# Reordering the start of a fused convolution and gated-MLP kernel: where loads, casts and hand-over marks stand, and two PSUM tiles for the last set

## The chip, the cores and the metric

One NeuronCore of a Trainium2 chip. The metric is device time in microseconds (us) of one execution; runs are compared on the same chip and in the same rounds. TensorE is "PE" in the profile, VectorE "DVE", ScalarE "ACT", GpSimd "POOL", SyncE's DMA queue "SPq".

## The reference

```python
def reference(x, weight, moe_w_in, moe_w_out):     # cut to what matters
    w = softmax(weight, axis=-1)                   # 8 heads, 7 taps
    # causal 7-tap convolution of x [8, 4096, 192], one weight row per group of 24 channels
    y = conv(x, w).reshape(32768, 192)
    h = y @ moe_w_in                               # 192 -> 2048
    return (h * cos(h)) @ moe_w_out                # 2048 -> 192
```

## The kernel before

Two batches of rows are worked at once, in the upper and lower 64 rows of the array. A string tells the order of work. Each letter is one step, and the recording keeps that order on every engine.

- `U`: 6 matmuls of 64x512 give one h tile (three PSUM tiles, of two banks each). `S`: its cosine on ACT. `M`: h times cosine on DVE, which frees the h tile.
- `d`: 8 matmuls of 64x192 into the two accumulators. Sixteen `d` make a set; `x`, `y` copy its two accumulators out.
- `C`, `c`, `e`: the two halves of a convolution pair on TensorE, then its eviction by ACT and its transposes on the DMA queue.
- `p`: GpSimd casts x for a later pair, and the x for the one after it is loaded.
- `k`: the next job of a list: casts of weights, loads.

Below, "the eleventh d" is the d with index 10 of the first set, and U16 is the first U of the second token tile. It needs the transposes of the second conv pair made in the fill.

The two halves of an accumulator pair change over at fixed d. A memset on GpSimd, the "mark", stands between, so that the matmuls on one half of the array wait for those on the other:

```python
    def changeover(end):
        ins = nc.gpsimd.memset(mark, 0.0)
        order(ins, end)                            # waits for the last matmul of the old side
        return ins                                 # the next d waits for it
    # ... in down(k, j), after step j:
        if j < 15 and TURNS[(j + 1) // 2][0] != flip:
            turns[k] = changeover(end)             # after steps 3, 9 and 13
```

The mark stands in GpSimd's program order, behind whatever cast was recorded before it (in the profile before it ran at 29.43 us, behind four casts begun at 27.63). The start, the "fill", and the end before the change:

```python
    load_w2(0)
    load_w2(1)                                     # both halves of w_out, early in the queue
    # ... cut ...
    def later():                                   # the jobs of "k"
        yield from (lambda q=q: cast_w1(1, q) for q in range(NCH))
        yield cast_pair
        yield from (lambda q=q: cast_w1(2, q) for q in range(NCH))
        yield cast_pair
        yield lambda: load_ahead(2)                # x for the third tile
        yield from (lambda q=q: cast_w1(3, q) for q in range(NCH))
        yield from (lambda c=c, q=q: cast_w2(c, q) for c in range(2) for q in range(4))
    # ... cut ...
    fill("kkkUSMUSMUSMkUSMUSMkkkUSCceMUSMUSMkUSMkUSCceMUSMkkkkkkkkkkkUSMU")
    emit("dddSMdUdMpSUdSdMUdSMdUdMSCcpUedSdMCcdedMUdpSdUyxUMS")
    for k in range(1, NSETS - 2):
        emit("dddSMdUdMSUdSdMUdSMdUdMSUdSdMCcdedMUdpSdUyxUMS")
    last = h_pool.tile([128, 2, T], FP32, name="h")
    last = [last[:, k, :] for k in range(2)]
    emit("dddMSdUdMSUdSdMUdSMdMM" + "tttt" + "dddddtttttt" + "ddxytttttt" + "xy")
```

## Time and profile before

| | before |
|---|---|
| time, median of 3 runs (range) | 723.93 us (723.11 to 724.34) |
| span of the profiled run | 721.9 us |
| TensorE busy in 40 to 710 us | 100% |
| TensorE idle in 10-20, 20-30, 30-40 us | 2.6, 2.6, 2.0 us |
| a set in steady state (first d to first d) | 10.9 us |

How to read it: a kernel whose TensorE is never idle for 670 us cannot win there by moving work. Only the first 40 us and the last 11 us can give anything.

### The profile page before, as it was taken

The page shows a single profiled execution, that of the slowest core. Times are in us where ns is not written, and L with a number is a line of the kernel's source. Part 1 is how long each engine was busy: PE and PEld are TensorE (multiplying, and loading weights), DVE is VectorE, ACT ScalarE, POOL GpSimd, SP SyncE. Part 2 cuts the span into 40 slices and gives each one's busy share as a digit, 9 for nine tenths or more (in the row PEclk, how much of TensorE's full clock was granted, in tenths as well). Part 3 has the DMA queues.
Part 4 walks back from the last instruction along what each step waited for, and adds up shares of the span by engine and source line. Part 5 has one row for each costly group of instructions (what it writes and reads, how often), then busy time and mean ns, then how long its engine had stood idle before and what let it go on. Part 6 is the DMA issues. An engine that isn't in the chain of part 4 may idle for free.

```text
span 721.9 us, 27691 instructions
## 1 busy us (share of the span) xinstructions
PE 707.8 (98%) x12370; PEld 527.0 (73%) x12370; DVE 640.9 (89%) x593; ACT 589.4 (82%) x641; POOL 95.0 (13%) x344
## 2 busy tenths in 40 slices
PE   7799999999999999999999999999999999999997
PEld 5477777777777777777777777777777777777776
DVE  5779899999889989898898998998998999999994
ACT  5788888888888888888888888888888888777773
POOL 4520111110110111111101111101101100000000
PEclk9999999999999999999999999999999999999999
DMA  9976443552616236254452352526253321011102
GB/s 227 248 120 151 87 93 93 115 132 63 158 40 157 75 83 158 66 126 109 120 121 77 94 136 83 138 59 158 50 146 85 84 62 55 25 45 46 46 24 67
DMA packets 126435, 72.58 MB, mean 101 GB/s; under 512 B 52524, under 2 KB 124780, under 8 KB 126316
## 3 DMA queue, kind: packets, MB, share of 16 engines
q1 hardware_dynamic: 125482, 70.23, 40.2%
q8 instruction: 96, 1.57, 0.9%
q10 hardware_dynamic: 834, 0.59, 0.3%
q14 instruction: 23, 0.19, 0.1%
HBM read 33.48 MB, written 25.17 MB: 81 GB/s over the span
## 4 chain that ended last, share of the span: by engine, by line
PE 95%; DMA 2%; DVE 1%; ACT 1%; issue 0%; ACTq 0%; POOL 0%; POOLq 0%
PE h L287 49%; PE acc L287 46%; DVE g L397 1%; DMA cT<-ct 1%; DMA xw<-in_x_dram 1%; ACT cos L392 0%; ACT ct L345 0%; POOL xb L161 0%; ACTq L80 0%; PE acc L487 0%; DVE osb L434 0%; ACT cT L490 0%; ACT osb L434 0%; ACT cT L491 0%; ACTq L104 0%
## 5 line engine op out<-in xcount | busy, mean ns | idle before, releaser
L397 DVE TENSOR_TENSOR g<-h,cos 128x1024 bf16<-128x1024 f32 x512 | 603.9, 1220 | 29.9 <-ACT cos L392 23.2
L392 ACT ACTIVATE cos<-h 128x1024 bf16<-128x1024 f32 x512 | 511.2, 1024 | 109.5 <-PE h L287 90.8
L287 PEld LDWEIGHTS <-g 64*128 64x128 bf16 x8192 | 353.4, 94 | 103.9 <-POOL mark L297 4.0
L287 PE MATMUL acc<-w,g 64*128 64x192 bf16 x8064 | 415.8, 243 | 1.2 <-POOL mark L297 1.2
L287 PE MATMUL h<-cT,w 64*128 64x512 bf16 x3072 | 407.0, 376 | 5.7 <-DVE g L397 3.4
L287 PEld LDWEIGHTS <-w 64*128 64x128 bf16 x3072 | 147.3, 94 | 82.6 <-issue 7.5
L297 POOL MEMSET mark<- 1x1 f32 x192 | 16.9, 88 | 601.4 <-PE acc L287 592.8
L434 DVE COPY osb<-acc 128x384 f32<-128x384 f32 x63 | 35.1, 558 | 40.2 <-PE acc L287 40.2
L161 POOL CAST xb<-xw 128x512 bf16<-128x512 f32 (+1 forms) x112 | 64.7, 607 | 15.6 <-DMA xw<-in_x_dram 14.4
L345 ACT CAST ct<-h 112x1024 bf16<-112x1024 f32 (+2 forms) x54 | 53.6, 992 | 6.0 <-PE h L287 2.4
L287 PE MATMUL h<-xb,band 64*128 64x192 bf16 (+11 forms) x940 | 34.9, 212 | 0.4 <-DVE xb L161 0.3
L434 ACT COPY osb<-acc 128x384 f32<-128x384 f32 x63 | 29.8, 473 | 5.7 <-PE acc L287 5.7
L287 PEld LDWEIGHTS <-band 64*128 64x128 bf16 x1008 | 31.6, 95 | 1.4 <-issue 1.0
L235 POOL CAST w<-xw 128x512 bf16<-128x512 f32 x12 | 7.0, 614 | 2.0 <-DMA xw<-in_moe_w_in_dram 1.9
L183 PE MATMUL acc<-unit 128*112 128x112 bf16 x76 | 5.8, 256 | 1.3 <-POOL unit L166 1.3
L183 PEld LDWEIGHTS <-unit 128*112 128x112 bf16 x76 | 5.6, 170 | 1.4 <-POOL unit L166 1.3
L287 PE MATMUL h<-w,g 64*128 64x192 bf16 x128 | 5.9, 243 | 0.3 <-POOL mark L297 0.3
L245 POOL CAST w<-xw 128x384 bf16<-128x384 f32 x8 | 3.7, 507 | 1.8 <-DMA xw<-in_moe_w_out_dram 1.8
L196 ACT ACT_TABLE_LOAD x1 | 1.3, 1283 | 2.6 <-issue 2.6
L216 ACT CAST band<-acc 128x448 bf16<-128x448 f32 x1 | 0.5, 532 | 2.7 <-PE acc L215 2.7
L434 DVE COPY osb<-h 128x384 f32<-128x384 f32 x1 | 0.6, 559 | 2.4 <-ACT osb L434 2.4
L161 DVE CAST xb<-xw 128x512 bf16<-128x512 f32 (+1 forms) x2 | 0.9, 485 | 1.4 <-DMA xw<-in_x_dram 1.4
(37 smaller groups left out, 19.9 us busy)
## 6 DMA issues: line engine op xcount, KB each, us to landing
out_dram<-osb SPq DMA_DIRECT2D x63, 384.0 KB, 2.6
xw<-in_x_dram SPq DMA_DIRECT2D x62, 384.0 KB, 6.9
xw<-in_x_dram SPq DMA_DIRECT2D x7, 336.0 KB, 4.4
xw<-in_moe_w_in_dram SPq DMA_DIRECT2D x4, 512.0 KB, 7.7
xw<-in_moe_w_out_dram SPq DMA_DIRECT2D x2, 768.0 KB, 6.4
cT<-ct SPq DMA_TRANSPOSE x68, 2.7
xw<-in_moe_w_in_dram SPq DMA_DIRECT2D x8, 128.0 KB, 7.0
xw<-in_x_dram SPq DMA_DIRECT2D x6, 96.0 KB, 6.8
```

Source lines behind the costliest of these rows:

```text
L161: copies[j % len(copies)](out=xbs[p][:, s0:s1], in_=src)
L183: nc.tensor.matmul(out=acc[0][0:W, 0:W], lhsT=unit, rhs=unit, start=True, stop=True)
L196: nc.scalar.activation(out=wex, in_=wq, func=AF.Exp)
L216: nc.scalar.copy(out=band[:, :, V:W], in_=spread)
L235: copy(out=w1[:, q, c * CW:(c + 1) * CW], in_=staged[1, c][:, q, :])
L245: nc.gpsimd.tensor_copy(out=w2[:, c * n:(c + 1) * n, :][:, fs, :], in_=staged[2, c][:, fs, :])
L287: ins = nc.tensor.matmul(out=o, lhsT=w, rhs=r, start=start, stop=stop, skip_group_check=True)
L297: ins = nc.gpsimd.memset(mark, 0.0)
L345: copy(out=ct[0:W, 0:n].rearrange("p j s c -> p s j c"), in_=ps[0:W, :, 0:n * L].rearrange("p s (j c) -> p s j c", c=L))
L392: nc.scalar.activation(out=cos, in_=hs[n], func=AF.Sin, bias=math.pi / 2.0, scale=1.0)
L397: nc.vector.tensor_tensor(out=g, in0=hs.pop(n), in1=cs.pop(n), op=ALU.mult)
L434: copy(out=osbs[k][:, 2 * bank:2 * bank + 2, :].rearrange("p a d -> p (a d)"), in_=src[:, 0:2 * D])
```

## The change

Intent: take away TensorE's waits in the fill. Half of w_out is loaded behind the first pair of transposes, x for the third tile behind the second pair. The second of two additional conv pairs moves from the first set to the second. In the last set the two accumulators get an h tile each, and three `d` are moved ahead of the last `U`.

```diff
     load_w2(0)
-    load_w2(1)
@@ later()
         yield cast_pair
-        yield lambda: load_ahead(2)
+        yield lambda: load_w2(1)
         yield from (lambda q=q: cast_w1(3, q) for q in range(NCH))
-        yield from (lambda c=c, q=q: cast_w2(c, q) for c in range(2) for q in range(4))
+        yield from (lambda q=q: cast_w2(0, q) for q in range(4))
+        yield lambda: load_ahead(2)
+        yield from (lambda q=q: cast_w2(1, q) for q in range(4))
@@
-    fill("kkkUSMUSMUSMkUSMUSMkkkUSCceMUSMUSMkUSMkUSCceMUSMkkkkkkkkkkkUSMU")
-    emit("dddSMdUdMpSUdSdMUdSMdUdMSCcpUedSdMCcdedMUdpSdUyxUMS")
-    for k in range(1, NSETS - 2):
+    fill("kkkUSMUSMUSMkUSMUSMkkkUSCceMUSMkUSMkUSMkkkUSCceMUSMkkkkkUSMU")
+    fill("dddSMdkkUdMkkSUdSdMUdSMdUpdMSUdSdMCcdedMUdpSdUyxUMS")
+    emit("dddSMdUdMSUdSdMUdSMdUdMSCcpUedSdMCcdedMUdpSdUyxUMS")
+    for _ in range(NSETS - 4):
         emit("dddSMdUdMSUdSdMUdSMdUdMSUdSdMCcdedMUdpSdUyxUMS")
-    last = h_pool.tile([128, 2, T], FP32, name="h")
-    last = [last[:, k, :] for k in range(2)]
-    emit("dddMSdUdMSUdSdMUdSMdMM" + "tttt" + "dddddtttttt" + "ddxytttttt" + "xy")
+    last = [h_pool.tile([128, 2, T], FP32, name="h")[:, 0, :] for _ in range(2)]
+    emit("dddMSdUdMSUdSdMdddUdSMdMM" + "tttt" + "ddtttttt" + "ddxytttttt" + "xy")
```

## The prediction

> **What bounds the kernel now.** I read the page first, then the table of windows, then waits, chain and timeline of the first 45 us and of the end. Letters are the kernel's own: U is one "up" block (6 matmuls of 64x512 into an h tile), S its cosine on ACT, M its product on DVE, d one "down" step (8 matmuls of 64x192), C/c the two halves of a convolution pair, e its eviction and transposes, p a cast of x. A set is 16 d. Columns of the windows are busy us per engine, then granted clock, DMA share, GB/s.
>
> ```profile
> PE 707.8 (98%) x12370; PEld 527.0 (73%) x12370; DVE 640.9 (89%) x593; ACT 589.4 (82%) x641; POOL 95.0 (13%) x344
> ...
> 10.00:20.00 10.00, 7.40 (x90) 3.93 (x92) 8.33 (x9) 7.88 (x11) 5.40 (x10) 1.00 1.08 262
> 20.00:30.00 10.00, 7.36 (x122) 4.32 (x120) 9.06 (x9) 8.59 (x11) 7.18 (x16) 1.00 1.15 286
> 30.00:40.00 10.00, 7.97 (x157) 6.02 (x155) 5.21 (x5) 5.15 (x6) 2.33 (x5) 0.83 1.17 197
> ...
> 100.00:200.00 100.00, 100.00 (x1742) 76.87 (x1740) 91.13 (x84) 84.75 (x93) 12.51 (x47) 1.00 0.43 105
> ```
>
> From 40 us to 710 us TensorE is never idle: nothing in the change can win there. What is loose is the fill (2.6 us idle in each of 10-20 and 20-30, 2.0 in 30-40, plus a lowered clock) and some 11 us at the end. The waits and the timeline of the fill say where:
>
> ```profile
> PE h L287 <- DMA cT<-ct: 2.0, 1, 2.0
> ...
> 27.63 1.86 POOL L245 CAST w<-xw 128x384 bf16<-128x384 f32 x4 [0.34 <-DMA xw<-in_moe_w_out_dram]
> 28.56 2.52 SPq L372 DMA_TRANSPOSE cT<-ct  x2
> 29.43 0.09 POOL L297 MEMSET mark<- 1x1 f32 x1
> 29.57 0.50 PE L287 MATMUL acc<-w,g 64*128 64x192 bf16 x8 [0.98 <-POOL mark L297]
> 32.58 1.17 POOL L161 CAST xb<-xw 128x512 bf16<-128x512 f32 x2 [3.06 <-DMA xw<-in_x_dram]
> 34.72 0.82 PE L287 MATMUL h<-cT,w 64*128 64x512 bf16 x6 [2.02 <-DMA cT<-ct]
> 36.27 0.09 POOL L297 MEMSET mark<- 1x1 f32 x1 [2.52 <-PE acc L287]
> ```
>
> The fifth d waits 0.98 us for a mark (a memset by which GpSimd hands the accumulator's halves over), which stood behind the w_out casts. The 17th U (U16, first of the second token tile) waits 2.02 us for transposes, issued only at 28.56, because four x loads for the third tile are issued at 25.81 ahead of them. Then the clock falls:
>
> ```profile
> 35.00:36.00 1.00, 1.00 (x17) 0.77 (x15) 0.00 (x0) 0.42 (x1) 0.00 (x0) 0.73 1.13 212
> 36.00:37.00 1.00, 1.00 (x32) 0.95 (x30) 0.36 (x1) 0.60 (x1) 0.71 (x3) 0.50 1.10 220
> 37.00:38.00 1.00, 1.00 (x7) 0.38 (x4) 0.86 (x1) 0.96 (x1) 0.44 (x1) 0.50 1.14 213
> 38.00:39.00 1.00, 1.00 (x16) 0.96 (x14) 0.00 (x0) 0.73 (x2) 0.00 (x0) 0.56 1.11 223
> ...
> 717.99 0.48 ACT L434 COPY osb<-h 128x384 f32<-128x384 f32 x1 [1.92 <-PE h L287]
> 718.50 0.56 DVE L434 COPY osb<-h 128x384 f32<-128x384 f32 x1 [2.39 <-ACT osb L434]
> ```
>
> 0.73, 0.50, 0.50, 0.56 are a half clock from about 35.46 to 38.87. The last two lines are the end: DVE's last copy waits for ACT's, though it reads another bank.
>
> [...] the 3.41 us before 35.46 were not wholly idle, only 2.0 us of them (40% busy)[...]; 11.56 to 14.98 was 62% busy and kept its clock. [...] transposes issued by 31.08 land around 35 because the x loads are ahead. [...]
>
> **The change part by part.**
> 1. *w_out's second half and its four casts go later.* The mark after the fourth d now stands ahead of those casts, after the first four, which end at 27.30; the fourth d ends at 27.95, so the mark is hidden under U13 (27.77 to 28.60). Gain 0.98 us. The second half is needed only at the ninth d.
> 2. *x for the third tile goes behind the second pair of transposes.* U16's wait goes. Check of the new rate: U13 ends 28.60, U14 after one d at about 28.9, U15 30.2, U16 at 31.6 instead of 34.72. U16 needs M13, which in the trace ends at 30.9. For the queue I work from the starts of consumers: w_out's halves land at 25.4 and 27.6, the x tile at 32.5, the transposes at about 35.0. A pair of transposes takes some 2.1 us of queue (estimate: 32.5 to 35.0 less a small x load). Order after: w_out 0, transposes, w_out 1, transposes, x. Transposes land near 30.5, before 31.6. Gain 2.03 us.
> 3. *The half clock after it.* Between 35.54 and 39.92 the chain has 0.60 for a d that costs 0.33, 2.14 for a conv half and a U that cost 1.45, 1.00 for two d that cost 0.66: 1.30 us lost, to be had back if the clock stays up.
> 4. *The x tile now lands later, and a mark stands behind its casts.* GpSimd's order after is: mark, four w_out casts, two casts of this x, mark for the eleventh d. All queue work that stood before the x tile still stands there and one pair of transposes is added: 32.46 + 2.1 = 34.5 (33.7 to 34.9). Two casts 1.17, mark and semaphores 0.2: the eleventh d can start near 35.9. Without that wait it would start at 33.3 (U16 31.6, d 0.33, U17 0.65 more, with M14 done at about 32.2). So a new TensorE stall of 2.6 us (1.9 to 3.0) takes the place of the old one.
> 5. *The clock again.* If windows lie as before (32.05 to 35.46), TensorE is idle from 33.3 to 35.46, 2.16 of 3.41 us, 37% busy, a little less than what halved the clock before. I give it 0.7. Cost: 35.9 to 38.87 at half speed, 1.5 us, so 1.05 in expectation.
> 6. *Second extra conv pair one set later.* Its matmuls (0.65 us for 40) leave the first set and come back in the second; total TensorE work is the same. In the second set each wait on M has 0.2 to 0.4 us of slack in steady state, so at most 0.2 us is lost there; after a stall DVE is ahead, so I take 0.
> 7. *The last set.* Two h tiles instead of one let DVE's last copy wait for TensorE and not for ACT: 718.50 becomes 717.99, gain 0.5. Three d moved ahead of the last U hide one exposed mark (711.14 to 711.39, 0.25), but that U ends at 709.6 instead of 708.7, its S and M (1.02 and 1.22) end near 712.1, and the d that needs it would come at 711.95: 0.2 given back. Two tiles leave U only one free h tile, but the last U waits for M508, ended at 707.4, and the first final-set step for M510, ended 709.98, both in time. Net 0.5.
>
> Sum: -0.98 - 2.03 - 1.30 + 2.6 + 1.05 + 0 - 0.5 = -1.16 us. 723.93 - 1.16 = 722.8. I shade it to 722.5, because step 4 rests on a queue estimate and errors there are more often in the new order's favour (the DMA queue was nearly idle for 1 us, at 33 to 34, in the old order; a queue without that pause lands x sooner).
>
> **The rivals.**
> A. *Clean gain.* x lands early enough (by 32, or the mark is reached otherwise) and steps 4 and 5 vanish: -4.3 - 0.5 = -4.8, 719.1 us. For it: that is evidently the intent, DMA moves 286 GB/s here and the old pause may go. Against: the x loads alone run at some 215 GB/s in the 1 us windows of this queue and cannot start before the transposes are through.
> B. *Stall without clock loss.* Step 4 as worked out, but the window straddles it[...]: -4.31 + 2.6 - 0.5 = -2.2, 721.7 us. For it: 62% busy kept the clock. Against: 37% is below the 40% that lost it.
> C. *Swap for nothing.* Stall of 3.0 with the clock halved, and a stall of a few tenths in the heavier second set: -4.31 + 3.0 + 1.5 + 0.3 - 0.2 = +0.3, 724.2 us. For it: the transposes of this trace have pauses of 1 us in them. Against: the tail gain is nearly certain.
> D. *DVE as the bound in the fill*: DVE is 9.06 of 10 busy in 20-30, so TensorE freed of its waits would catch up with M. Against: U14 to U17 need M11 to M14, ended at about 28.5, 29.6, 30.9 and 32.2, each 0.3 us or more before its U.
>
> **Range and chances.** The centre is between the expected sum and B. Eight times in ten I expect 720.2 to 724.0: the low end is a stall of about 1 us and a kept clock, the high end rival C. The whole fill idle after 11.85 us is 6.5 us, under 1%, so 2% (14.5 us) either way could come only from something I have not seen: 0.01 faster, 0.98 within, 0.01 slower.
>
> **What would show it.** Step 1: the fifth d starts before 29.0 with no wait on a mark. Step 2: U16 starts at about 31.6 with no wait on transposes. Step 4: the waits name the mark before the eleventh d, 1.9 to 3.0 us, with the x cast just before it starting at 34 to 35. Step 5: the clock column is 0.5 from about 35.5 to 38.9. Step 6: TensorE 100% busy in the second set. Step 7: the last ACT and DVE copies start together, and the end follows 0.5 us sooner. Wrong would be: no stall at the eleventh d (rival A), or a half clock anywhere else in the fill, or U idle for h tiles in the last set.

The forecast's sum came to -1.16 us, 722.8, shaded to 722.5. That a stretch with little TensorE work brings a half clock, and the chance of 0.7 in step 5, were estimates from the one profile of before: about 40% busy in 32.05 to 35.46 us, ahead of the half clock, and 62% in 11.56 to 14.98, after which the clock stayed full. Step 5's "windows" are such stretches of 3.41 us.

## The result, and the profile after

The changed kernel took 722.12 us (median of 4; 721.75 to 723.30) against 724.13 us for the kernel before (4 runs), ratio 0.9975, 95% interval 0.9957 to 0.9994. A repetition of five rounds on another chip gave 723.02 against 724.38 us, ratio 0.9979 (0.9966 to 0.9991). A ratio here is the mean time of one kernel's fast runs over that of the other's of the same rounds, so it is not quite the ratio of the medians.

The windows of the changed kernel (busy us of PE, PEld, DVE, ACT, POOL; then granted clock, DMA share, GB/s), to be held against those of before:

```profile
10.00:20.00 10.00, 7.46 (x91) 3.97 (x90) 8.29 (x9) 7.83 (x11) 4.88 (x9) 1.00 1.08 259
20.00:30.00 10.00, 8.69 (x132) 4.66 (x129) 8.31 (x8) 8.42 (x11) 6.72 (x15) 1.00 1.17 255
30.00:40.00 10.00, 7.57 (x126) 5.51 (x123) 5.87 (x5) 5.09 (x6) 2.90 (x8) 0.84 1.10 241
```

TensorE gained 1.3 us of work in 20-30 and lost 0.4 us in 30-40. The timeline of the changed kernel's fill shows why (start, duration, instruction; in brackets the idle time before it and what ended it):

```profile
28.43 0.09 POOL L296 MEMSET mark<- 1x1 f32 x1 [0.62 <-PE acc L286]
28.83 0.51 PE L286 MATMUL acc<-w,g 64*128 64x192 bf16 x8
28.87 1.86 POOL L245 CAST w<-xw 128x384 bf16<-128x384 f32 x4 [0.35 <-DMA xw<-in_moe_w_out_dram]
31.78 0.83 PE L286 MATMUL h<-cT,w 64*128 64x512 bf16 x6
34.75 1.17 POOL L161 CAST xb<-xw 128x512 bf16<-128x512 f32 x2 [4.03 <-DMA xw<-in_x_dram]
35.86 0.09 POOL L296 MEMSET mark<- 1x1 f32 x1
36.01 0.83 PE L286 MATMUL acc<-w,g 64*128 64x192 bf16 x16 [2.43 <-POOL mark L296]
```

Both old waits are gone: the fifth d at 28.83 and U16 at 31.78 have no bracket. A new one of 2.43 us stands at 36.01. Read it upwards: TensorE waits for the mark, the mark came 1.1 us after the casts of x began, and those had waited 4.03 us for the x load to land. The wait is labelled with the mark, but the load ended it.

Why the load came late can be read on SyncE's queue, which issues one transfer after another (start, duration of the issue):

```profile
25.04 2.69 SPq L371 DMA_TRANSPOSE cT<-ct  x2
27.82 6.26 SPq L110 DMA_DIRECT2D xw<-in_x_dram  x8
```

The first x load for the third tile is issued at 27.82 us, when the second pair of transposes has been issued. In the kernel before it was issued at 25.81. The cast of x starts 6.9 us after this issue in the changed kernel and 6.8 us in the kernel before, so the 2.0 us by which the issue moved are nearly all of the 2.2 us by which the cast moved. The data of the transposes did not fill that time: their 784 packets passed in 0.78 us (28.39 to 29.17), the first packets of x followed at 29.26, and from 29.5 to 30.0 us the DMA share was 0.32. This is a reading of the traces; no run tests it.

The granted clock of the changed kernel, in one-microsecond windows behind that wait:

```profile
36.00:37.00 1.00, 0.99 (x30) 0.99 (x32) 0.06 (x1) 0.00 (x0) 0.00 (x0) 0.91 1.14 227
37.00:38.00 1.00, 1.00 (x30) 0.98 (x28) 0.00 (x0) 0.36 (x1) 0.00 (x0) 0.50 1.11 239
...
40.00:41.00 1.00, 1.00 (x22) 0.88 (x20) 0.04 (x1) 0.80 (x1) 0.18 (x1) 0.88 1.15 199
```

Worked back from 0.91 and 0.88, the clock was halved from 36.83 to 40.24: again 3.41 us, 1.37 us later than in the profile before. The timeline of the changed kernel's end:

```profile
717.57 0.56 DVE L433 COPY osb<-h 128x384 f32<-128x384 f32 x1 [1.87 <-PE h L286]
717.60 0.48 ACT L433 COPY osb<-h 128x384 f32<-128x384 f32 x1 [1.95 <-PE h L286]
718.11 0.50 ACTq L442 DMA_DIRECT2D out_dram<-osb  x1
```

The two copies now run side by side, each released by TensorE. From the first d of the last set but one (704.39 us before, 704.35 us after) to the end of the span, the profile of before has 17.49 us, the changed one 17.16: 0.33 us less.

### The profile page after: what moved, and what is told of

The parts are those of the page before. It is cut to its first block, busy times and chain, and to the rows that moved or that the text cites. A ratio compares the mean times of both kernels' runs of the same rounds, so it can differ in the third digit from the quotient of the medians.

```text
span 721.5 us, 27691 instructions
## 1 busy us (share of the span) xinstructions
PE 709.0 (98%) x12370; PEld 522.5 (72%) x12370; DVE 640.7 (89%) x593; ACT 589.1 (82%) x641; POOL 95.0 (13%) x344
## 3 DMA queue, kind: packets, MB, share of 16 engines
q8 instruction: 96, 1.57, 0.9%
## 4 chain that ended last, share of the span: by engine, by line
PE 94%; DMA 4%; DVE 1%; SPq 0%; POOL 0%; issue 0%; ACT 0%; POOLq 0%
PE h L286 48%; PE acc L286 46%; DMA xw<-in_moe_w_in_dram 2%; DMA xw<-in_moe_w_out_dram 1%; DMA xw<-in_x_dram 1%; DVE g L396 0%; SPq L110 0%; POOL w L245 0%; ACT cos L391 0%; POOL xb L161 0%; DVE osb L433 0%; SPq L104 0%; POOLq L545 0%; POOL mark L296 0%; SPq L240 0%
## 5 line engine op out<-in xcount | busy, mean ns | idle before, releaser
L286 PEld LDWEIGHTS <-w 64*128 64x128 bf16 x3072 | 143.6, 94 | 82.8 <-issue 5.4
L286 PE MATMUL h<-xb,band 64*128 64x192 bf16 (+11 forms) x940 | 34.5, 212 | 0.0
L342 ACT CAST ct<-acc 112x512 bf16<-112x512 f32 (+1 forms) x4 | 2.0, 562 | 0.2 <-PE acc L286 0.2
```

Of the source, the lines that this page charges most:

```text
L286: ins = nc.tensor.matmul(out=o, lhsT=w, rhs=r, start=start, stop=stop, skip_group_check=True)
L342: copy(out=ct[0:W, 0:n, s, :], in_=bank[0:W, 0:n * L].rearrange("p (j c) -> p j c", c=L))
```

## The experiments

All twelve were correct and ran in five rounds. "x lands" below is read as the start of the cast that waited for it.

### The two halves of the change alone: e1_tail_only and e2_fill_only

```diff
 # e1: the kernel before, with only
+    last = [h_pool.tile([128, 2, T], FP32, name="h")[:, 0, :] for _ in range(2)]
+    emit("dddMSdUdMSUdSdMdddUdSMdMM" + "tttt" + "ddtttttt" + "ddxytttttt" + "xy")
 # e2: the changed kernel, with the two lines of before in their place
```

> The kernel before with the changed last set alone (two h tiles, three d moved ahead of the last U). My theory (the end gains some 0.4 us because the last DVE copy no longer waits for ACT's, and no more because the last store lands only 0.4 us sooner): 0.3 to 0.6 us faster than before, and in its profile the two last copies start within 0.1 us of each other. Rival (the whole measured gain of about 1.8 us is in the end): 1.5 us or more faster. Rival (one free h tile slows the last set): no gain.

> The changed kernel with the old last set. My theory (the fill trades its two old waits for one new wait of about 2.5 us before the eleventh d, and gains 1.4 us only when the clock is not halved after it): 0.2 us faster than before in runs whose mean clock is 0.996 to 0.997, about 1.4 to 1.8 us faster in runs whose clock is 0.999 or more; the mean 0.7 to 1.6 us faster. Rival (the gain is in the end alone): same as before within 0.3 us.

Measured: e1 723.00 us, ratio 0.9992 (0.9978 to 1.0006); e2 722.65, ratio 0.9989 (0.9975 to 1.0003); before 723.41. Neither alone is clear of noise; the two gains together (0.0008 and 0.0011 of the time) are near what the whole change showed. In the profiles the end is sharper than in the times: from the first d of the last set but one to the end, e1 takes 17.16 us (as the changed kernel) and e2 17.48 (as before). So the last set is worth 0.33 us, at the low edge of what I expected. The rest of e1's time difference is within the noise.

The profiles of these two happened to fall in runs without a half clock, so they show the fill without it. The waits of TensorE in 25.7 to 65 us, e1 first (who waited for whom: us in total, times, longest), then e2:

```profile
PE h L287 <- DMA cT<-ct: 2.0, 1, 2.0
PE acc L287 <- POOL mark L297: 1.1, 1, 1.1
PE h L287 <- DVE g L397: 0.5, 2, 0.3
PE acc L287 <- POOL w L245: 0.3, 1, 0.3
```

```profile
PE acc L286 <- POOL mark L296: 2.4, 1, 2.4
PE h L286 <- DVE g L396: 0.3, 1, 0.3
```

The trade is plain: 2.0 + 1.1 us of waits became one of 2.4. From the start of U13 (the U just ahead of the fifth d) to the first d of the fourth set, which holds the same work in all of these kernels, e1 takes 36.01 us and e2 34.95, both at full clock: 1.06 us less. With one half clock in each, the kernel before takes 37.04 us and the changed one 36.59 (36.43 in e5, below).

Counted from U12 (just ahead of the first d), before and changed show no gain in their profiles (39.00 and 39.11 us). U12 to U13 takes 1.96 us where nothing waits, as in before and e2, but 2.52 in the changed kernel's profile and 2.78 in e1's: there the first four d wait for the casts of w_out's first half. This early wait differs from run to run. It is in four of the ten profiles with w_out's second half moved and in one of the four without; whether the new order makes it more frequent stays open.

My expectation for e2 spoke of runs at a mean clock of 0.996 to 0.997, and there were none. Of its three runs at 0.998 two were the slow ones (723.80 and 723.34), but 721.90 was at 0.998 too.

### Is the new wait the x load, or GpSimd's order? e3_conv_later, e8_cast_after_mark, e9_conv_at_end

```diff
 # e3: no conv pair in the first set; two in each of the next two
-    fill("dddSMdkkUdMkkSUdSdMUdSMdUpdMSUdSdMCcdedMUdpSdUyxUMS")
+    fill("dddSMdkkUdMkkSUdSdMUdSMdUdMSUdSdMddMUdpSdUyxUMS")
+    emit("dddSMdUdMSUdSdMUdSMdUdMSCcpUedSdMCcdedMUdpSdUyxUMS")
 # (and one plain set fewer)
 # e8: the cast of x one step later, behind the eleventh d's mark
+    fill("dddSMdkkUdMkkSUdSdMUdSMdUdpMSUdSdMCcdedMUdpSdUyxUMS")
 # e9: as e8, and the conv pair at the end of the set
+    fill("dddSMdkkUdMkkSUdSdMUdSMdUdpMSUdSdMddMUdpSdCceUyxUMS")
```

> The changed kernel without any conv pair in the first set: x's cast stands behind that set's last mark, and the second and third set have two conv pairs each. My theory (the wait at the eleventh d is the mark behind the x cast, whose load lands near 34.5 us): the wait vanishes, the clock stays up in every run, the first set ends some 2.5 us earlier besides the conv work moved, and the kernel is 2.0 to 3.5 us faster than the changed one (about 719.2). Rival (TensorE would wait for something else there anyway, M or the h tiles, as DVE is nearly full in the fill): less than 0.8 us faster. Rival (two sets with two conv pairs give it back as waits of TensorE on DVE): TensorE not 100% busy in 50 to 75 us.

> The changed kernel with the cast of x for the first set's conv pair put behind the mark of the eleventh d on GpSimd. Theory (the wait is for x; the mark only hands it on): the eleventh and twelfth d run without a wait at 33.5 us, then TensorE waits as long, for the same cast, before the conv half: 1.7 to 2.1 us of wait at about 36.0; the set ends 0.6 us sooner than in the changed kernel. Rival (the order on GpSimd is itself the cause): no wait left, 2 us or more faster than the changed kernel.

> The changed kernel with the cast of x behind the mark of the eleventh d, and the first set's conv pair moved to that set's end, behind the sixteenth d. Theory (x lands near 34.5 to 35.5 us whatever stands around it; with more TensorE work ahead of its first user the wait shrinks by that work): TensorE's wait for the x cast falls from 2.4 us to 0 to 0.4 us, no half clock, 2.0 to 3.0 us faster than the changed kernel, 0.995 to 0.9945 of before. Rival (TensorE then waits for M or an h tile instead, because the pair takes an h tile just where U needs it): waits on M of 1 us or more in the first set, not faster than 0.996.

| | median us | before, same chip | ratio (95%) |
|---|---|---|---|
| e3_conv_later | 720.45 | 723.41 | 0.9956 (0.9943 to 0.9970) |
| e8_cast_after_mark | 721.15 | 724.38 | 0.9958 (0.9946 to 0.9971) |
| e9_conv_at_end | 720.42 | 723.27 | 0.9967 (0.9953 to 0.9980) |

e8's timeline, where only GpSimd's order was changed:

```profile
33.56 0.09 POOL L296 MEMSET mark<- 1x1 f32 x1 [2.15 <-PE acc L286]
33.91 0.84 PE L286 MATMUL acc<-w,g 64*128 64x192 bf16 x16
35.50 1.17 POOL L161 CAST xb<-xw 128x512 bf16<-128x512 f32 x2 [1.85 <-DMA xw<-in_x_dram]
36.16 0.40 PE L286 MATMUL h<-xb,band 64*128 64x96 bf16 x12 [1.42 <-POOL xb L161]
36.72 0.44 PE L286 MATMUL h<-xb,band 64*128 64x32 bf16 x16 [0.15 <-POOL xb L161]
```

The eleventh d runs at 33.91 without a wait, and the conv half waits 1.42 + 0.15 us for the same cast. So the load is the cause, as the theory has it, and the order on GpSimd is worth about 0.9 us of the 2.43: two d of work done meanwhile (0.66), and the conv half starts at the first cast where the mark needed both. I had expected 1.7 to 2.1 us of wait; 1.57 is less. The time fell by more than that, from 723.02 to 721.15 us on one chip. Some of this may be the clock, which one run of five of e8 shows at 0.998 or less and two of five of the changed kernel; that was not separated.

In e9 the waits of TensorE in 25.7 to 65 us are:

```profile
PE h L286 <- DVE g L396: 0.9, 2, 0.6
PE acc L286 <- POOL mark L296: 0.5, 1, 0.5
```

The x wait is gone entirely. What is left is half of the rival's: 0.6 us for M, because the pair takes an h tile just there, and 0.5 us for the last mark, now behind two casts. From the start of U13 to the first d of the fourth set (the same work in all of these) e3 takes 32.98 us, e9 33.85, e8 34.30, e2 34.95. e3's two crowded sets cost it 0.52 us of idle TensorE. Its profile is of the slowest of its five runs, and before U13 the first four d waited for the casts of w_out, so that U12 to U13 took 3.76 us:

```profile
PE acc L286 <- POOL w L245: 1.2, 1, 1.2
```

Counted from U12 that hides e3's gain: e9 35.86 us, e3 36.74, e8 36.88, e2 36.91.

Two gains that I had expected were too large: e3 was to be 2.0 to 3.5 us faster than the changed kernel and is some 1.5 us faster by the ratios; e9 was to reach 0.995 of before and has 0.9967. The three intervals overlap, so which of the three is best stays open; each has a lower ratio than either measurement of the changed kernel. e8 and the changed kernel were timed on the same chip, and even there the two intervals just overlap.

### The changed kernel again: e5_after_again

No edit.

> The changed kernel once more, on the chip of the next three. Theory: 0.5 to 2.0 us faster than before; if its profile falls in a run without a halved clock, the eleventh d starts near 36 us with a wait of 2.2 to 2.9 us, and the next set 4.4 us after it (6.0 in the first profile, with the clock halved). Rival (the first result of 1.8 us was luck of a few runs): within 0.4 us of before.

Measured: 723.02 us, ratio 0.9979. Its profile fell in a run with a halved clock again. The eleventh d starts at 36.80 after 2.4 us, and the next set 5.90 us later; in e2, without the half clock, it was 4.44 us. So the half clock there cost 1.5 us.

### The parts of the fill alone: e6_wout_only and e7_x_only

```diff
 # e6: the kernel before, with w_out's second half loaded by a job and its casts behind the mark
+        yield lambda: load_w2(1)
         yield lambda: load_ahead(2)
 # e7: the kernel before, with the x loads behind the second transposes
-        yield lambda: load_ahead(2)
         yield from (... cast_w1(3, q) ...)
         yield from (... cast_w2(c, q) ...)
+        yield lambda: load_ahead(2)
```

> The kernel before with w_out's second half and its casts moved, and nothing else. Theory (gains before a later wait for data are swallowed by it): the fifth d no longer waits for the mark (0.98 us gone), but U16 still waits for transposes behind the x loads and starts at the same 34.7 to 35.5 us after a wait of some 3 us: same as before within 0.3 us. Rival (the terms add, as my prediction's sum had them): 1.0 us faster.

> The kernel before with the x loads of the third tile moved behind the second transposes, and nothing else. Theory (the x load's landing sets the eleventh d whatever is before it): the fifth d still waits 0.9 to 1.0 us for its mark, U16 does not wait, the eleventh d or the conv pair waits for x at the same 35.5 to 36.2 us as in the changed kernel, the wait there shorter by that 1 us: as fast as the changed kernel without its last set, 0.4 to 1.0 us faster than before. Rival (the w_out part is needed for the gain): same as before, or slower.

e6: 724.34 us, ratio 1.0000 (0.9987 to 1.0012). Its timeline:

```profile
28.61 0.51 PE L286 MATMUL acc<-w,g 64*128 64x192 bf16 x8
32.90 1.17 POOL L161 CAST xb<-xw 128x512 bf16<-128x512 f32 x2 [1.13 <-DMA xw<-in_x_dram]
34.76 1.06 PE L286 MATMUL h<-cT,w 64*128 64x512 bf16 x6 [3.03 <-DMA cT<-ct]
```

Almost a microsecond saved at the fifth d (28.61 for 29.57) reappears in full at U16: the wait there grew from 2.02 to 3.03 us and U16 starts at 34.76, where it was 34.72. A saving ahead of a wait for data is no saving.

e7: 725.27 us, ratio 1.0004 (0.9990 to 1.0018). The gain of 0.4 to 1.0 us that I expected did not come. With both conv pairs still in the first set, one of them stands before U17, and it is this that waits for x (2.1 us in the profile), so U17 and the ACT and DVE work behind it are held up too; and a second wait on a mark (0.3 us) appears in the next set, behind the cast of the next x. The profile has two halved windows in it, so I do not take a sum from it. The fifth d did not wait for its mark as I had expected (30.50, no bracket): in this profile the fill's beginning was late, with U12 at 27.70. That the place of the second conv pair matters is what these lines suggest; it was not isolated.

### The clock: e4_warm and e12_before_warm

```diff
+            elif op == "w":                       # 32 in e4, 28 in e12; nobody reads the result
+                idle = h_pool.tile([128, 2, T], FP32, name="h")
+                for _ in range(32):
+                    nc.tensor.matmul(out=idle[0:W, 0, 0:W], lhsT=unit, rhs=unit, start=True, stop=True)
 # e4, in the changed kernel before the eleventh d: "...UpdMSUwdSdM..."
 # e12, in the kernel before, ahead of U16: "...UdSMdwUdM..."
```

> The changed kernel with 32 matmuls that nobody reads (about 1.8 us) put into the new wait before the eleventh d, in a free h tile. My theory (part of the runs lose 1.3 to 1.5 us because this wait lets the clock fall[...]): every run has a mean clock of 0.999 or more, no run is above 722.4 us, the mean is 0.3 to 1.0 us below the changed kernel's and the spread is smaller. Rival (the fall of the clock has another cause, or costs nothing because ACT and DVE bound that stretch): some runs still at 0.996 to 0.997, or no difference in time; if the added matmuls delay what follows, slower by up to 0.5 us.

> The kernel before with 28 unread matmuls (about 1.7 us) in the wait of U16. Theory (a third of the runs of before lose 1.2 us to a halved clock after that wait, the others do not): no run with a mean clock of 0.997 or below from this place, U16 no later, the mean 0.2 to 0.6 us below before. Rival (as with the same filler in the changed kernel, the added instructions cost some 0.6 us of their own elsewhere): not faster than before.

Measured: e4 723.33 us, ratio 1.0000 (0.9987 to 1.0013); e12 724.83, ratio 1.0019 (1.0006 to 1.0032). e12 is slower than the kernel before. e4's ratio is above both of the changed kernel's, which were taken on other chips, with intervals that overlap; two of its five runs were at 0.998. So neither filler gained. In their profiles no half clock follows the filled wait, and in e4 the stretch from the eleventh d to the next set takes 4.43 us, nearly the 4.44 of e2. But a wait of TensorE that neither kernel had without filler appears in the next set, with no releaser in the profile ("issue"). In e12's waits it is:

```profile
PE acc L287 <- issue: 1.3, 1, 1.3
```

It is 0.6 us in e4. Its cause stays open; as a way to price the clock by total time the two runs failed.

What the traces do show of the clock is when it changed. In the profile of before the first full clock comes at 4.74 us and the half clock at 35.46, in that of the changed kernel at 6.11 and 36.83: in both 30.72 us later, nine times 3.41, and the half clock lasts 3.41 us. In the fourteen profiles (those of before, of the changed kernel and of the twelve experiments) the first full clock comes at 4.5 to 7.2 us, and later changes lie whole multiples of 3.41 us after it. So I divided each profile, from its first full clock on, into stretches of 3.41 us, called windows here, and read TensorE's busy share of each. Up to 40 us:

| busy share of a window | how many | half clock in the next window |
|---|---|---|
| 0.14 to 0.41 (before 0.41, changed 0.29, e5 0.36, e6 0.14, e7 0.38, e10 0.41) | 6 | all 6 |
| 0.44 to 0.47 (e4, e7, e10) | 3 | 2 of 3 |
| 0.50 and more | all others | none |

These are counts in fourteen profiles; they do not show why the clock fell.

The changed kernel and e2 have the same stall of 2.4 us. In the changed kernel 2.4 us of it lay within one window (33.41 to 36.83, 29% busy). In e2 a window's edge at 34.39 cut it in two, the emptier window was 61% busy, and the clock stayed up. So the same stall was followed by a half clock in one profile and not in the other; of nine runs of the changed kernel three had a mean clock of 0.998 or less (0.996, 0.998, 0.998).

The same reading goes with a late beginning of the fill in three profiles. In e4, e7 and e10 the first conv pair of the fill found its x late, the window around it was 0.41 to 0.47 busy, and the clock fell there, at 19 to 23 us; in these three U12 starts at 27.5 to 27.7 us, in the others at 25.7 to 26.6. e4's two windows, the second at half clock:

```profile
15.89:19.30 3.41, 1.59 (x18) 0.62 (x16) 3.41 (x4) 2.63 (x3) 0.78 (x2) 1.00 1.09 238
19.30:22.72 3.42, 3.41 (x42) 1.71 (x41) 0.89 (x1) 2.10 (x3) 2.61 (x6) 0.50 1.01 258
```

So a low mean clock in a timed run says that a window was halved, not which one: e4's profile, at 0.998, had its half clock at 19.30, not behind the stall that its filler was put into.

### Can x land sooner? e10_x_two_queues and e11_both

```diff
-        yield lambda: load_ahead(2)
+        yield lambda: load_ahead(2, (nc.sync, nc.scalar))
 # e10: in the changed kernel; e11: in e9
```

> The changed kernel with the x loads of the third tile issued on two queues, one per half of the partitions. Theory (in the new order x lands late because its two halves, of 64 partitions each, pass one after the other at some 215 GB/s behind both transposes): the x cast starts 1.2 to 2.0 us sooner, the wait before the eleventh d falls to 0.5 to 1.2 us, U16 still does not wait, 1.0 to 2.0 us faster than the changed kernel. Rival (DMA is full whatever the queue): the x cast starts within 0.5 us of before and transposes land later, so U16 waits again; no gain.

> Both of the last two edits. Theory: little over the conv pair at the end alone, since that leaves only 0 to 0.4 us of wait: within 0.4 us of it. Rival (early set waits on transposes or w_out casts move too): different by over 0.8 us either way.

e10: 724.65 us, ratio 1.0018 (1.0005 to 1.0031); e11: 722.38 us, ratio 0.9990 (0.9978 to 1.0003), 2 us slower than e9 beside it. What the rival foretold came true. e10's timeline:

```profile
35.36 0.82 PE L286 MATMUL h<-cT,w 64*128 64x512 bf16 x6 [1.90 <-DMA cT<-ct]
37.27 1.17 POOL L161 CAST xb<-xw 128x512 bf16<-128x512 f32 x2 [5.41 <-DMA xw<-in_x_dram]
38.53 0.67 PE L286 MATMUL acc<-w,g 64*128 64x192 bf16 x12 [1.37 <-POOL mark L296]
```

U16 waits for transposes again (1.90 us), now that half of x is issued on the other queue. And x is no sooner: its cast starts 8.9 us after the first d (28.37), against 8.2 us in the changed kernel (34.75 less 26.51). The rival's reason, that DMA is full, is not shown: from 34 to 35 us the DMA share in e10 was 0.48. SyncE issues its half of x at 29.58 us, behind the transposes as before, and the cast needs both halves. Issuing all of x on the other queue was not tried.

## Why the prediction was right or wrong

The prediction was 722.5 us, 720.2 to 724.0, and no change clear of 2%. Measured: 722.12 and 723.02 us. By its own steps:

1. *The fifth d's mark* (gain 0.98): right in place. It starts at 28.83 without a wait. As a gain by itself it is nothing: e6 shows that U16's wait swallows it. The sum was right only because step 2 removed that wait.
2. *U16's transposes* (gain 2.03): right. U16 at 31.78 (31.6 predicted), with no wait.
3. *The half clock given back* (gain 1.30): mis-sized as a term of the sum. In size it is about right: from U16 to the second set e1 takes 7.10 us at full clock, before 8.28 at half, 1.18 us. But I took it as always present, from one profile. Of 27 runs of the kernel before in the experiments 8 had a mean clock of 0.998 or less, which is what one halved window leaves (half of 3.41 us, in 722; and it may have lain elsewhere). If each of these lost 1.2 us here, the mean loss was 0.35 us.
4. *x lands later, behind the transposes, with a mark behind its casts* (cost 2.6): right in place and in size. x landed at 34.7 (34.5), the eleventh d started at 36.01 (35.9), the wait was 2.4 us. e8 and e9 show that the load was its cause. That the size fits is in part luck. The 2.1 us for a pair of transposes were read from a pair with a pause in it; in the changed kernel the same pair passed in 0.78 us, and what moved x was that it was issued 2.0 us later.
5. *The clock falls again* (0.7 times 1.5): the size was right, 1.5 us (5.90 and 6.04 us against 4.44 for the same work). The half clock came at 36.83 and not at 35.5, because the windows did not lie as before (the first full clock came at 6.11 and not at 4.74). The chance was too high for the runs as a whole: 3 of 9 had a mean clock of 0.998 or less (about +0.5 us in the mean). Steps 3 and 5 erred in opposite directions, so their sum, -0.25 predicted, comes out near +0.15.
6. *The conv pair one set later* (0): right; TensorE was idle 0.1 us in 40 to 50 us, and fully busy after it.
7. *The last set* (gain 0.5): 0.33. The copies gained more than I had worked out (they end 0.89 us sooner counted from the same d), and TensorE's part 0.37 us of it, but the last stores gave back 0.56: both are now issued at 718.1 together, and ACT's lands last, at 720.61, 2.5 us after its issue, where the last one of before took 1.95.

Of the rivals, A (a clean gain) fell: x landed at 34.7 and not by 32. B (a stall without clock loss) is what e2's profile shows, and the main line is what both profiles of the changed kernel show. C (a swap for nothing) did not occur: both ratios are below 1, and the heavier second set lost 0.1 us. D (DVE as the bound) did not either: TensorE's waits on M in this stretch are 0.3 us, as before.

With measured sizes the terms make about -0.8 us: waits 3.0 to 2.4 us, clock +0.15, end -0.33. The two measurements say -1.8 and -1.5 us with intervals that reach -0.4 and -0.65, so -0.8 lies inside both. Counted directly in the profiles, from U13 to the fourth set and over the end, the gain is 0.8 to 0.9 us between kernels that both had a half clock (0.45 or 0.61, and 0.33) and 1.4 us between e1's fill and e2's at full clock (1.06 and 0.33). What of the remaining difference is real is open: the beginning of the fill, which the change hardly touches, by itself varies by 2 us (U12 at 25.67 to 27.72 us). That the predicted 722.5 us came so near is in part luck: two terms with opposite errors, and a shading of 0.3 us by hand.

The change moved the time little because what it removed was not a bound but an order: on SyncE's queue, putting the second pair of transposes forward (25.04 us for 28.56) put the x load back (27.82 for 25.81). About a microsecond more was to be had by giving the late load's user more work ahead of it (e3, e8, e9).

## What to carry to other kernels

Where many transfers share one queue, ask of every transfer that is moved what it now stands behind, when it will be issued, and who waits for the one put back; then place independent work ahead of that user. A hand-over step (here a one-element memset on GpSimd) can inherit the wait of what was recorded before it: in the changed kernel the mark ran at 35.86 us, behind a cast that had waited 4.03 us for its load, and in e8, ahead of that cast, at 33.56. So a cast that waits for a load should stand behind the mark. One profile is one draw: an effect that comes in some runs only (a mean clock of 0.998 or less in 3 of 9 runs of the changed kernel) must be counted over runs before it goes into a sum.

## What these traces show of the hardware

- A stall of 2.0 us (before) and one of 2.4 us (the changed kernel), each within one window of 3.41 us, were followed by a half clock of 3.41 us; e2's stall of 2.4 us, cut in two by a window's edge, was not.
- The packets of a pair of DMA transposes (784 of 256 bytes, 0.20 MB) passed in 0.78 us in the changed kernel, 257 GB/s; with a pause in between, in the kernel before, the same pair took 2.2 us. A transpose held SyncE's queue for 1.2 to 2.4 us in the changed kernel (median 1.24), one x load for a median of 0.62.
- Unread filler matmuls were followed, several microseconds later, by a TensorE wait of 0.6 us (e4) and 1.3 us (e12) without a releaser in the profile.
